# Attention and a gated MLP in one kernel: half of the transposes moved from the matrix engine to DMA

## The chip, the cores and the metric

The kernel runs on one core of one Trainium2 chip. A core has a matrix engine (TensorE, "PE" in the profile, with "PEld" for its weight loads), VectorE (DVE), ScalarE (ACT), GpSimd (POOL) and SyncE (SP), which work in parallel, each through its own instructions in program order. SP, ACT and POOL issue DMA transfers, which 16 DMA engines carry out. Matrix products land in PSUM, and DVE or ACT copy them from there to SBUF.

The metric is the time of one execution on the device in microseconds: 181.52 us as the median of three runs (181.5 to 182.01). The profiled execution spans 179.5 us.

## What is computed

Four batch items ("items one to four", b = 0 to 3 in the code), eight heads, 768 tokens, head dimension 64. Each head's sequence is cut into 8 blocks of 96. A small matrix P per head mixes the blocks of k and v; then each block attends only to itself. The result x goes through an MLP with the maximum of two branches.

```python
P = sort_net                                   # (4, 8, 8, 8)
for _ in range(5):                             # softmax over rows, then columns to sum 1
    P = np.exp(P - P.max(-1, keepdims=True))
    P = P / (P.sum(-1, keepdims=True) + 1e-09)
    P = P / (P.sum(-2, keepdims=True) + 1e-09)
k_sorted = np.einsum('bhij,bhjcd->bhicd', P, k_b)   # blocks of 96 tokens
v_sorted = np.einsum('bhij,bhjcd->bhicd', P, v_b)
scores = q_b @ k_sorted.transpose / sqrt(64)        # 96 x 96 per block
attn = softmax(scores);  x = attn @ v_sorted        # (3072 tokens, 512)
h1, h2 = x @ w1, x @ w2                             # 512 -> 1024
out = np.maximum(h1, h2) @ w_out                    # 1024 -> 512, float32
```

The kernel uses max(h1, h2) = relu(x(w1 - w2)) + x w2, and multiplies w2 by w_out once (wc). So the output of a tile is eight products with g = relu(...) and four with x itself.

## The kernel before

Products contract over partitions, so q and x are needed transposed. q is loaded as 128 partitions of 6 tokens each (token = 6 p + r). Two heads are put side by side by two DVE copies (pair_q; not for item one), and a transpose of 128 x 128 through PE then gives both heads' queries at once. Its result is copied out of PSUM into qT:

```python
def q_transposes(b, half, eng=None):
    if half == 0:
        qT[b] = qpool.tile([128, HP, R, 128], BF16, tag="qT", name="qT")
    ps = ps_bf16("tq_ps")
    for n in range(2 * R):                     # R = 6: 12 transposes
        hp, r = half * 2 + n // R, n % R
        c = slice(n * 128, (n + 1) * 128)
        if b in q_pair:
            nc.tensor.matmul(ps[:, c], q_pair[b][:, hp, r], ident, is_transpose=True, ...)
            continue
        ...                                    # item one: one head at a time
    evac(qT[b][:, half * 2 : half * 2 + 2]..., ps[:, 0 : 2 * R * 128], 2 * R * 128, two_x=True, eng=eng)
```

Queries of a block stand in qT in the order (r, c), not in token order (c, r). The scores of unit u (four blocks of two heads) and their exponential keep that order:

```python
def scores(b, u, n=0):
    ih, hp = divmod(u, HP)
    ps = ps_f32("s_ps")
    for ii in range(4):
        for h2 in range(2):
            rhs = qT[b][rows, hp, :, i * PB : (i + 1) * PB]      # 6 x 16 queries
            nc.tensor.matmul(ps[:, h2 * 512 + ii * BLK : h2 * 512 + (ii + 1) * BLK], kT[b]..., rhs, ...)
    nc.scalar.activation(out=e[:, 0 : 8 * BLK]..., in_=ps[0:BLK]..., func=AF.Exp, scale=scale)
```

values(b, u) multiplies e with v (the row sum comes along as a column of ones) and divides on DVE: one reciprocal, one multiplication that writes a half of a tile x (three buffers). When two units have filled x, x_transposes(b, t) transposes it in eight blocks on PE; only the copy into xT brings the tokens of a block into their order:

```python
def x_transposes(b, t, eng=None):
    ih, hh = divmod(t, 2)
    ps = ps_bf16("tx_ps")
    x = x_tiles.pop((b, ih, hh))
    for m in range(8):
        h2, ii = divmod(m, 4)
        nc.tensor.matmul(ps[:, h2 * 1024 + ii * BLK : ...], x[:, h2, ii]..., ident[0:BLK, 0:BLK],
                         is_transpose=True, ...)
    dst = xT[:, b % 2, ih, hh].rearrange("p h (i c r) -> p h i c r", r=R, c=PB)
    src = ps....rearrange("p h (i r c) -> p h i c r", r=R, c=PB)
    evac(dst, src, 2 * TCH, eng=eng)
```

`evac` and `pick` give a copy to ACT or DVE by a running estimate of their loads. All PSUM tiles (4 KB per partition) share four buffers.

The order of work is written by hand. For each item there are "units" of the MLP, and between them "steps" of the next item's attention. Units 0 to 3 (moe_h of channel half 0) read xT of groups t = 0 and 1; units 4 to 7 (half 1) read groups t = 2 and 3; then moe_out makes the outputs, and SP stores 256 tokens (512 KB) at a time. `tail` holds what is left over from the attention of the item whose MLP begins:

```python
elif b == 1:                                   # prepares item three during the MLP of item two
    vs = [lambda t=t: sort_v_pair(2, t) for t in range(8)]
    steps = group(*pairs) + group(*ks) + qs[:1] + group(*SC[0:2], vs[0]) + qs[1:]
    steps += group(*vs[1:4]) + group(*vs[4:7]) + group(*SC[2:4], vs[7]) + VA[:2]
else:                                          # b == 2
    steps = group(*pairs) + group(*ks) + qs + group(*SC[0:2])
    steps += group(*SC[2:5]) + VA[:2]
rest = SC[4:] if b == 1 else SC[5:]
steps += VA[2:3] + TR[:1] + VA[3:4]
steps += group(*rest[:-1]) + TR[1:2] + VA[4:5] + rest[-1:] + VA[5:6]
...                                            # steps from unit 2 on, spread evenly over the units
tail = {0: [VA[6]], 1: [TR[2], VA[7]], 2: [TR[3]]}    # after unit 0, 1, 2 of the next item
```

SC, VA and TR are the scores, values and x_transposes of the item; qs are the two halves of q_transposes, pairs the two pair_q copies, ks the sorts of k. q_raw has one buffer: the load of the next item's q waits for the pairing copies.

Of the kernel before, what the change touches and what calls it, by code (L numbers as in the profile page):

```python
# [15 lines left out]
def kernel(  # L16
# [16 lines left out]
    nc = tc.nc  # L33
# [6 lines left out]
    BLK = S // NB  # L40
# [5 lines left out]
    R = S // 128  # L46
    PB = 128 // NB
    HP = H // 2
    HB = BLK // 2
    TCH = S // 2  # L50
# [14 lines left out]
    def ps_f32(name):  # L65
        return psum.tile([128, 1024], FP32, tag="ps", name=name)

    def ps_bf16(name):
        return psum.tile([128, 2048], BF16, tag="ps", name=name)
# [21 lines left out]
    def pick(a_ns, d_ns):  # L91
        if load["A"] + a_ns <= load["D"] + d_ns:
            load["A"] += a_ns
            return "A"
        load["D"] += d_ns
        return "D"

    def evac(out_ap, in_ap, n, two_x=False, eng=None):
        a_ns, d_ns = (200 + n) / 1.2, (130 + (n / 2 if two_x else n)) / 0.96
        if eng:  # L100
            load[eng] += a_ns if eng == "A" else d_ns
        if (eng or pick(a_ns, d_ns)) == "A":
            nc.scalar.copy(out=out_ap, in_=in_ap)  # L103
        else:
            nc.vector.tensor_copy(out=out_ap, in_=in_ap)  # L105
# [5 lines left out]
    q_raw, qT = {}, {}  # L111
# [10 lines left out]
    for n in range(NE):  # L122
        t = big.tile([BLK, 8 * BLK + 32], BF16, tag=f"e{n}", name=f"e{n}")
# [194 lines left out]
    xT = big.tile([128, 2, 2, 2, 2, TCH], BF16, tag="xT", name="xT")  # L318

    q_pair = {}  # L320
# [11 lines left out]
    def q_transposes(b, half, eng=None):  # L332

        if half == 0:
            qT[b] = qpool.tile([128, HP, R, 128], BF16, tag="qT", name="qT")
        ps = ps_bf16("tq_ps")
        for n in range(2 * R):
            hp, r = half * 2 + n // R, n % R
            c = slice(n * 128, (n + 1) * 128)
            if b in q_pair:  # L340
                nc.tensor.matmul(  # L341
                    ps[:, c], q_pair[b][:, hp, r], ident, is_transpose=True, start=True, stop=True
                )
                continue
            for h2 in range(2):
                nc.tensor.matmul(
                    ps[h2 * 64 : h2 * 64 + 64, c],
                    q_raw[b][:, hp + 4 * h2, r * D : (r + 1) * D],
                    ident,
                    is_transpose=True,  # L350
                    start=True,
                    stop=True,
                )
        evac(
            qT[b][:, half * 2 : half * 2 + 2].rearrange("p h r c -> p (h r c)"),
            ps[:, 0 : 2 * R * 128],
            2 * R * 128,
            two_x=True,
            eng=eng,
        )  # L360
# [66 lines left out]
    e_tiles, x_tiles = {}, {}  # L427
# [4 lines that stand above are left out]
        keep_streaming(ps, n)  # L432
        for ii in range(4):
            i = ih * 4 + ii
            for h2 in range(2):
                rows = slice(h2 * 64, h2 * 64 + 64)
                rhs = qT[b][rows, hp, :, i * PB : (i + 1) * PB]
                nc.tensor.matmul(  # L438
                    ps[:, h2 * 512 + ii * BLK : h2 * 512 + (ii + 1) * BLK],
                    kT[b][rows, (hp * 8 + i) * BLK : (hp * 8 + i) * BLK + 128],  # L440
                    rhs,
                    start=True,
                    stop=True,
                )
        e = e_bufs[(b * 8 + u) % NE]
        nc.scalar.activation(  # L446
            out=e[:, 0 : 8 * BLK].rearrange("p (t f) -> p t f", t=2),
            in_=ps[0:BLK].rearrange("p (t f) -> p t f", t=2)[:, :, 0 : 4 * BLK],
            func=AF.Exp,
            scale=scale,  # L450
        )
        load["A"] += 800
        e_tiles[b, u] = e
# [34 lines left out]
    def x_transposes(b, t, eng=None):  # L488

        ih, hh = divmod(t, 2)  # L490
        ps = ps_bf16("tx_ps")
        x = x_tiles.pop((b, ih, hh))
        for m in range(8):
            h2, ii = divmod(m, 4)
            nc.tensor.matmul(  # L495
                ps[:, h2 * 1024 + ii * BLK : h2 * 1024 + (ii + 1) * BLK],
                x[:, h2, ii].rearrange("p n d -> p (n d)"),
                ident[0:BLK, 0:BLK],
                is_transpose=True,
                start=True,  # L500
                stop=True,
            )

        dst = xT[:, b % 2, ih, hh].rearrange("p h (i c r) -> p h i c r", r=R, c=PB)
        src = ps.rearrange("p (h f) -> p h f", h=2)[:, :, 0:TCH].rearrange(
            "p h (i r c) -> p h i c r", r=R, c=PB
        )
        evac(dst, src, 2 * TCH, eng=eng)


    w2T = big.tile([128, NFB, DMODEL], BF16, tag="w2T", name="w2T")
# [144 lines left out]
    SC, VA, TR = att(0)  # L656
# [37 lines left out]
    def load_rest():  # L694
# [3 lines left out]
    tail = {  # L698
        0: [VA[4]],
        1: [SC[6], SC[7], VA[5]],  # L700
        2: [VA[6], TR[2], VA[7]],
        3: [TR[3], lambda: w2_transposes(1, "A")(), load_rest, lambda: block_diagonals(1)],
        4: [lambda: block_diagonals(2), lambda: turn(second, 0)],
        5: [lambda: block_diagonals(3), lambda: turn(second, 24)],
        6: [lambda: turn(second, 48)],
        7: [lambda: turn(second, 72)],
# [8 lines left out]
    for b in range(B):  # L715
        units = [lambda t=t: moe_h(b, 0, t, None if b else "A") for t in range(4)]
        if b == 0:
            units[0] = lambda: None
            units[1] = lambda: None
        units += [lambda t=t: moe_h(b, 1, t) for t in range(4)]  # L720
        cost = [1.3] * 8
        if b == 0:
            units += [lambda dmt=dmt: w_product(dmt) for dmt in range(4)]
            cost += [1.7] * 4
        units += [
            lambda ti=ti, part=part: moe_out(b, ti, part)
            for ti in range(6 if b < B - 1 else 4)
            for part in range(2)
        ]
        cost += [1.3] * 12  # L730
        if b == B - 1:
            units += [
                lambda: moe_out_last(4, [(0, 512, "D")]),
                lambda: moe_out_last(5, [(0, 256, "A"), (256, 384, "D"), (384, 512, "A")]),
            ]
        steps, lo = [], 2
        if b < B - 1:
            qs = [lambda half=half: q_transposes(b + 1, half) for half in range(2)]
            pairs = [lambda two=two: pair_q(b + 1, two) for two in range(2)]
            ks = [lambda t=t, b=b: sort_k(b + 1, t) for t in range(3)]  # L740
            SC, VA, TR = att(b + 1)

            def group(*fs):
                return [lambda: [f() for f in fs]]

            if b == 0:
                lo = 9
                tail[7] += ks
                vs = [lambda t=t: sort_v(1, t) for t in range(4)]
                for m, c in enumerate((0, 24, 48, 72)):  # L750
                    VA[m + 1 : m + 2] = group(VA[m + 1], lambda c=c: turn(both, c))
                steps = group(*vs[:3]) + qs[:1] + group(*SC[0:2], vs[3]) + qs[1:] + VA[:1]
                steps += group(*SC[2:5]) + VA[1:2]
            elif b == 1:
                vs = [lambda t=t: sort_v_pair(2, t) for t in range(8)]
                steps = group(*pairs) + group(*ks) + qs[:1] + group(*SC[0:2], vs[0]) + qs[1:]
                steps += group(*vs[1:4]) + group(*vs[4:7]) + group(*SC[2:4], vs[7]) + VA[:2]
            else:
                steps = group(*pairs) + group(*ks) + qs + group(*SC[0:2])
                steps += group(*SC[2:5]) + VA[:2]  # L760
            rest = SC[4:] if b == 1 else SC[5:]
            steps += VA[2:3] + TR[:1] + VA[3:4]
            steps += group(*rest[:-1]) + TR[1:2] + VA[4:5] + rest[-1:] + VA[5:6]
        done = 0
        for n, unit in enumerate(units):
            unit()
            for step in tail.get(n, []):
                step()
            total = sum(cost[lo:-2])
            want = -(-len(steps) * sum(cost[lo : n + 1]) // total)  # L770
            while done < min(want, len(steps)):
                steps[done]()
                done += 1
        tail = {0: [VA[6]], 1: [TR[2], VA[7]], 2: [TR[3]]}
        if b == 0:
            tail[3] = [lambda: load_k(3)]
            tail[8] = [lambda: load_q(3)]
# [28 lines left out]
```

The softmax here doesn't subtract the row's maximum and nothing guards it: scores larger than these inputs give would overflow.

## Time and profile before

| | before |
|---|---|
| time, median of 3 | 181.52 us |
| span of the profiled execution | 179.5 us |
| x transposes on PE (tile tx_ps) | 128 matmuls in 16 groups |
| q transposes on PE (tile tq_ps) | 48 for item one, 72 for items two to four |
| copies tx_ps to xT | 11 on ACT (797 ns), 5 on DVE (957 ns) |
| copies tq_ps to qT | 7 on DVE (958 ns), 1 on ACT (1439 ns) |
| exponentials | 32 on ACT, 804 ns each |
| issues of DMA on SP | sort_net, 11 outputs of 512 KB, two smaller ones |

How to read the profile: a line such as "L495 PE MATMUL tx_ps<-ident,x" names the kernel's line, the engine, the operation, and output and inputs. Line 495 is the transpose of x, 341 that of paired q, 438 the scores, 446 the exponential, 463 the values, 474 and 480 the reciprocal and the multiplication that makes x, 563 the first products of the MLP (h), 579 the relu on DVE, 590 the output products, 326 the pairing copy, 209 the copies of v into its working layout. Busy times of PE are modelled at a matmul's end, so single matmuls overlap: eight in a row take less than eight times the mean of one. "The chain that ended last" is the work that set the end, followed back from the last instruction.

### The profile page before, as it was taken

To read this page: it belongs to the slowest core of one execution; us is meant where nothing else is said; L and a number is where in the kernel's file an instruction comes from. 1 tells how busy PE (TensorE), PEld (TensorE's weight loads), DVE (VectorE), ACT (ScalarE), POOL (GpSimd) and SP (SyncE) were. 2 spreads that over 40 slices of the span, in tenths; PEclk is the share of its full clock that TensorE was granted. 3 is DMA by queue.
4 is the path that set the end of the run, shared out by engine and by line. 5 is a ranking of instruction groups with operands and counts; after the bars stand their busy time and mean duration, and the time that the engine had idled before them with its cause. 6 is when DMAs were issued, how large, how long until landed. Compare 5 with 4: busy or idle time off the path is not lost.

```text
span 179.5 us, 4648 instructions
## 1 busy us (share of the span) xinstructions
PE 170.0 (95%) x2083; PEld 100.7 (56%) x2083; DVE 94.0 (52%) x192; ACT 91.8 (51%) x110; POOL 22.9 (13%) x39
## 2 busy tenths in 40 slices
PE   7797989999999989999989999999999999999993
PEld 2246666666565535577655554657555546554453
DVE  5878498559864395253586436156245415340210
ACT  3695876777664445368784341465833233520021
POOL 7861443200180000001000000000000000000000
PEclk9999999999999999999999999999999999999999
DMA  3999999999299991235600113200001132000333
GB/s 58 201 204 206 200 207 214 194 202 208 55 120 221 206 250 48 99 117 74 108 4 0 57 63 117 104 17 5 0 4 42 74 117 116 4 0 4 117 117 117
DMA packets 13939, 19.17 MB, mean 107 GB/s; under 512 B 800, under 2 KB 8864, under 8 KB 13920
## 3 DMA queue, kind: packets, MB, share of 16 engines
q0 software_dynamic: 10304, 12.58, 41.6%
q1 hardware_dynamic: 3328, 6.10, 8.9%
q8 instruction: 16, 0.26, 0.6%
q10 hardware_dynamic: 288, 0.20, 0.3%
q14 instruction: 3, 0.02, 0.0%
HBM read 25.17 MB, written 6.29 MB: 175 GB/s over the span
## 4 chain that ended last, share of the span: by engine, by line
PE 58%; DMA 29%; DVE 5%; issue 4%; POOL 2%; ACT 1%; POOLq 0%; DVEq 0%
PE out_ps L590 32%; PE h_ps L563 16%; DMA v_raw<-in_v_dram 10%; DMA w_sb<-in_moe_w_dram 10%; DMA q_raw<-in_q_dram 9%; PE o_ps L463 3%; PE tx_ps L495 2%; PE k_ps L371 2%; PE s_ps L438 2%; DVE g L579 2%; PE tq_ps L341 1%; DVE x L480 1%; DVE xT L105 1%; POOL v_raw L153 1%; DVE v_dc L209 1%
## 5 line engine op out<-in xcount | busy, mean ns | idle before, releaser
L590 PE MATMUL out_ps<-wo_sb,g 128*128 128x512 bf16 (+2 forms) x208 | 48.1, 363 | 0.2 <-DVE g L579 0.2
L563 PE MATMUL h_ps<-xT,w_sb 128*128 128x384 bf16 x256 | 46.1, 326 | 0.5 <-DVE g L579 0.2
L563 PEld LDWEIGHTS <-w_sb 128*128 128x128 bf16 x256 | 23.6, 97 | 15.1 <-issue 0.7
L577 ACT ACTIVATE g<-h_ps 128x768 bf16<-128x768 f32 x24 | 19.4, 811 | 23.4 <-PE h_ps L563 23.4
L446 ACT ACTIVATE e<-s_ps 96x768 bf16<-96x768 f32 x32 | 24.1, 804 | 14.0 <-PE s_ps L438 13.9
L590 PEld LDWEIGHTS <-g 128*128 128x128 bf16 x208 | 17.7, 97 | 15.8 <-issue 0.2
L590 PE MATMUL out_ps<-wc,xT 128*128 128x512 bf16 (+2 forms) x104 | 25.0, 362 | 0.0
L103 ACT COPY o<-out_ps 128x1024 f32<-128x1024 f32 x8 | 8.1, 1012 | 31.0 <-PE out_ps L590 27.3
L480 DVE TENSOR_TENSOR x<-o_ps,rs 96x512 bf16<-96x512 f32 x32 | 22.0, 687 | 1.1
L474 DVE RECIPROCAL rs<-o_ps 96x8 f32<-96x8 f32 x32 | 6.4, 201 | 27.4 <-PE o_ps L463 27.2
L590 PEld LDWEIGHTS <-xT 128*128 128x128 bf16 x104 | 9.9, 98 | 10.9
L209 DVE COPY v_dc<-v_raw 64x1536 bf16<-64x1536 bf16 (+2 forms) x9 | 14.1, 1583 | 1.8 <-DMA v_raw<-in_v_dram 1.7
L463 PEld LDWEIGHTS <-e 96*128 96x128 bf16 x256 | 11.2, 98 | 6.5 <-DVE x L480 1.1
L579 DVE TENSOR_SCALAR g<-h_ps 128x768 bf16<-128x768 f32 x8 | 7.7, 958 | 13.5 <-PE h_ps L563 10.6
L463 PE MATMUL o_ps<-v_sb,e 96*128 96x65 bf16 x256 | 12.9, 193 | 1.3 <-DVE x L480 0.6
L105 DVE CAST v_sb<-v_ps 96x1024 bf16<-96x1024 f32 x7 | 8.5, 1217 | 5.9 <-PE v_ps L392 3.9
L103 ACT CAST v_sb<-v_ps 96x1024 bf16<-96x1024 f32 x9 | 8.7, 1010 | 3.4 <-PE v_ps L392 2.6
L103 ACT CAST kT<-k_ps 128x1024 bf16<-128x1024 f32 x10 | 9.5, 1024 | 0.0
L103 ACT COPY xT<-tx_ps 128x768 bf16<-128x768 bf16 x11 | 8.8, 797 | 1.5 <-PE tx_ps L495 1.5
L438 PEld LDWEIGHTS <-kT 64*128 64x128 bf16 x256 | 6.2, 94 | 5.4 <-issue 4.4
L129 POOL DMA_DIRECT2D q_raw<-in_q_dram x4 | 3.6, 901 | 43.0 <-DVE q_pair L326 40.7
L438 PE MATMUL s_ps<-qT,kT 64*128 64x96 bf16 x256 | 9.0, 204 | 0.1
(78 smaller groups left out, 162.5 us busy)
## 6 DMA issues: line engine op xcount, KB each, us to landing
out_dram<-o SPq DMA_DIRECT2D x11, 512.0 KB, 2.8
k_raw<-in_k_dram POOLq DMA_DIRECT2D x12, 256.0 KB, 13.7
q_raw<-in_q_dram POOLq DMA_DIRECT2D x4, 768.0 KB, 8.9
v_raw<-in_v_dram POOLq DMA_DIRECT2D x6, 384.0 KB, 12.0
w_sb<-in_moe_w_dram POOLq DMA_DIRECT2D x3, 512.0 KB, 15.7
wo_sb<-in_moe_w_out_dram POOLq DMA_DIRECT2D x2, 512.0 KB, 19.9
v_raw<-in_v_dram POOLq DMA_DIRECT2D x3, 256.0 KB, 5.1
w_sb<-in_moe_w_dram POOLq DMA_DIRECT2D x2, 256.0 KB, 14.3
```

The costliest lines, as they stand in the source:

```text
L103: nc.scalar.copy(out=out_ap, in_=in_ap)
L105: nc.vector.tensor_copy(out=out_ap, in_=in_ap)
L209: nc.vector.tensor_copy(out=dst, in_=src)
L438: nc.tensor.matmul(ps[:, h2 * 512 + ii * BLK : h2 * 512 + (ii + 1) * BLK], kT[b][rows, (hp * 8 + i) * BLK : (hp * 8 + i) * BLK + 128], rhs ...
L446: nc.scalar.activation(out=e[:, 0 : 8 * BLK].rearrange("p (t f) -> p t f", t=2), in_=ps[0:BLK].rearrange("p (t f) -> p t f", t=2)[:, :, 0 ...
L463: nc.tensor.matmul(ps[:, h2 * 512 + ii * 65 : h2 * 512 + (ii + 1) * 65], e[:, (h2 * 4 + ii) * BLK : (h2 * 4 + ii) * BLK + 128], v_sb[:, m0 ...
L474: nc.vector.reciprocal(out=rs, in_=ov[:, :, :, 64])
L480: nc.vector.tensor_tensor(out=x, in0=ov[:, :, :, 0:D], in1=rs.to_broadcast([BLK, 2, 4, D]), op=ALU.mult,)
L563: nc.tensor.matmul(h_ps[t][:, m * 512 : m * 512 + TCH], w1_sb[:, hp, fb * 128 : (fb + 1) * 128], xT[:, b % 2, ch, hp % 2, hp // 2, :], sta ...
L577: nc.scalar.activation(out=g, in_=src, func=AF.Relu)
L579: nc.vector.tensor_scalar(out=g, in0=src, scalar1=0.0, scalar2=None, op0=ALU.max)
L590: nc.tensor.matmul(dst, g_tiles[b, ch, m // 2][:, m % 2, off : off + 128] if m < NFB else xT[:, b % 2, ch, hp % 2, hp // 2, off : off + 12 ...
```

## The change

The transposes of x for items two to four, and of q for items three and four, are taken from PE and done by DMA: one transfer transposes a whole group and writes straight to xT or qT, so that PSUM and the copy out of it are not needed. The transfers go on SP's queue, among the outputs. [...]the order is now mended earlier: the exponential reads PSUM in token order, and e, x and xT have that order for all items. The scores of a block move to 128 columns each, so that the exponential's pattern has one stride for all eight blocks.

To give the transfers time, pairing and q transposes move to the start of an item's MLP (after unit 0), the sorts of v stand ahead of the first scores, and one values unit (VA[6]) moves ahead of the border between items. Item one keeps both transposes on PE, and item two its q.

```diff
 def q_transposes(b, half, eng=None):
     if half == 0:
         qT[b] = qpool.tile([128, HP, R, 128], BF16, tag="qT", name="qT")
+    if b > 1:
+        hps = slice(half * 2, half * 2 + 2)
+        nc.sync.dma_start_transpose(
+            out=qT[b][:, hps].rearrange("p h r c -> p (h r) c"),
+            in_=q_pair[b][:, hps].rearrange("p h r d -> p (h r d)"),
+        )
+        return
 ... scores:
-                    ps[:, h2 * 512 + ii * BLK : h2 * 512 + (ii + 1) * BLK],
+                    ps[:, h2 * 512 + ii * 128 : h2 * 512 + ii * 128 + BLK],
 ...
-            out=e[:, 0 : 8 * BLK].rearrange("p (t f) -> p t f", t=2),
-            in_=ps[0:BLK].rearrange("p (t f) -> p t f", t=2)[:, :, 0 : 4 * BLK],
+            out=e[:, 0 : 8 * BLK].rearrange("p (t c r) -> p t c r", t=8, r=R),
+            in_=ps[0:BLK]
+            .rearrange("p (t f) -> p t f", t=8)[:, :, 0:BLK]
+            .rearrange("p t (r c) -> p t c r", r=R),
 ... x_transposes:
+        x = x_tiles.pop((b, ih, hh))
+        if b:
+            nc.sync.dma_start_transpose(
+                out=xT[:, b % 2, ih, hh].rearrange("p h (i c) -> p (h i) c", c=BLK),
+                in_=x.rearrange("p t i n d -> p (t i n d)"),
+            )
+            return
 ... (item one: the copy to xT is now contiguous on both sides, two_x=True)
 ... order of work, b == 1:
-                steps = group(*pairs) + group(*ks) + qs[:1] + group(*SC[0:2], vs[0]) + qs[1:]
-                steps += group(*vs[1:4]) + group(*vs[4:7]) + group(*SC[2:4], vs[7]) + VA[:2]
+                tail[0] = pairs + qs + tail[0]
+                steps = group(*ks) + group(*vs[1:4]) + group(*SC[0:2], vs[0])
+                steps += group(*vs[4:7]) + group(*SC[2:4], vs[7]) + VA[:2]
 ... b == 2:
-                steps = group(*pairs) + group(*ks) + qs + group(*SC[0:2])
+                tail[0] = pairs + qs + tail[0]
+                steps = group(*ks) + group(*SC[0:2])
 ... all items but the last:
-            steps += group(*rest[:-1]) + TR[1:2] + VA[4:5] + rest[-1:] + VA[5:6]
+            steps += group(*rest[:-1]) + TR[1:2] + VA[4:5] + rest[-1:] + VA[5:7]
 ...
-        tail = {0: [VA[6]], 1: [TR[2], VA[7]], 2: [TR[3]]}
+        tail = {0: [TR[2], VA[7]], 1: [TR[3]]}
```

More of the change, by code (lines that the diff above doesn't have):

```diff
@@ L490, in x_transposes @@
         ih, hh = divmod(t, 2)
+        x = x_tiles.pop((b, ih, hh))
[5 more added lines that the diff above has]
+            return
         ps = ps_bf16("tx_ps")
-        x = x_tiles.pop((b, ih, hh))
         for m in range(8):
@@ L495, in x_transposes @@
             nc.tensor.matmul(
-                ps[:, h2 * 1024 + ii * BLK : h2 * 1024 + (ii + 1) * BLK],
+                ps[:, m * BLK : (m + 1) * BLK],
                 x[:, h2, ii].rearrange("p n d -> p (n d)"),
@@ L502, in x_transposes @@
             )
-        dst = xT[:, b % 2, ih, hh].rearrange("p h (i c r) -> p h i c r", r=R, c=PB)
-        src = ps.rearrange("p (h f) -> p h f", h=2)[:, :, 0:TCH].rearrange(
-            "p h (i r c) -> p h i c r", r=R, c=PB
+        evac(
+            xT[:, b % 2, ih, hh].rearrange("p h f -> p (h f)"),
+            ps[:, 0 : 2 * TCH],
+            2 * TCH,
+            two_x=True,
+            eng=eng,
         )
-        evac(dst, src, 2 * TCH, eng=eng)
     w2T = big.tile([128, NFB, DMODEL], BF16, tag="w2T", name="w2T")
```

## The prediction

> **What bounds the kernel now.** I read the page's busy table first, then the chain that ended last in order of time, then a table of stages, then the tile view of the transposes and the list of DMA issues. The page says that TensorE (PE) is the busy engine, and that VectorE (DVE) and ScalarE (ACT) are about half idle:
>
> ```profile
> PE 170.0 (95%) x2083; PEld 100.7 (56%) x2083; DVE 94.0 (52%) x192; ACT 91.8 (51%) x110; POOL 22.9 (13%) x39
> ```
>
> An average hides stages, so next the stages (columns: stretch and its length, then busy us and instruction count of PE, weight loads, DVE, ACT, GpSimd, then clock, DMA share, GB/s):
>
> ```profile
> 62.00:95.00 33.00, 31.77 (x463) 19.48 (x461) 19.93 (x26) 20.89 (x24) 0.90 (x1) 1.00 0.44 99
> 95.00:131.00 36.00, 35.40 (x462) 21.32 (x462) 16.44 (x28) 18.34 (x24) 0.00 (x0) 1.00 0.12 45
> 131.00:155.00 24.00, 23.66 (x211) 12.96 (x210) 10.74 (x19) 7.87 (x11) 0.00 (x0) 1.00 0.18 67
> ...
> 64.00:161.00 97.00, 95.04 (x1155) 56.55 (x1156) 47.06 (x72) 47.46 (x57) 0.90 (x1) 1.00 0.22 63
> ```
>
> From 64 to 161 us PE is idle for only 97.00 - 95.04 = 1.96 us. So a matmul that disappears there should shorten the kernel by its own pipelined time, as long as no wait takes its place. Before 62 us the chain runs through loads from HBM; the last is v of items three and four, behind which DVE stands still for 1.72 us (to 62.00). What is saved before that point is mostly lost.
>
> The chain shows what the transposes cost (columns: start us, us, what). Around the border between items three and four:
>
> ```profile
> 115.00 1.30 PE h_ps L563 x8
> 116.31 0.36 PE tx_ps L495 x8
> 116.68 0.96 DVE xT L105
> 117.64 0.12 DVE rs L474
> 117.79 0.70 DVE x L480
> 118.53 0.51 PE tx_ps L495 x8
> 119.05 1.30 PE h_ps L563 x8
> 120.35 1.63 PE k_ps L371 x96
> 121.98 1.41 PE h_ps L563 x8
> 123.39 1.34 PE tq_ps L341 x24
> ```
>
> A group of eight x transposes holds PE for 0.34 us where it stands elsewhere in the chain (0.36 here, with a wait behind it). The q transposes of one item hold it for 1.34 us, 0.67 per half. The stretch from 116.68 to 118.53 is not all idle (another matmul group ran beside it): the timeline gives 0.34 us of PE idle ahead of the second x group, and the same again at 154.10.
>
> **What the Trainium skill says.** "VectorE: DVE Perf Modes", section "The three transpose paths", gives 390 ns for a 128x128 transpose on TensorE and 1309 ns through the DMA crossbar. The trace agrees that one alone is slow on PE (203 to 219 ns each by the tile view), but pipelined it is 0.67/12 = 56 ns, so the DMA path is not a saving of latency, only of PE time. "DMA: Bandwidth & Descriptors", section "Latency and other measured facts", gives 261 GB/s for a DMA transpose with a non-contiguous middle dimension, 350 to 400 where contiguous. The kernel before has no such transfer, so no trace here shows it. The same page, "Queues, rings and completion order", says that transfers issued by SP share one ring on each DMA engine, taken in order, and that an engine goes round robin between queues by packet. The trace fits: a 512 KB output takes 2.8 us alone and 6.1 us when it meets the loads. "TensorE: Matmul & The Clock Gate", section "Part 1: The HAM clock gate", warns that PE idle for about 3.4 us halves its clock; the trace shows a clock of 1.00 in every stage, so it has not yet been put to the test.
>
> **The change part by part.**
>
> *PE loses work.* Of 16 x groups 12 go: 12 x 0.34 = 4.1 us. Of eight q halves four go: 4 x 0.67 = 2.7 us. The instruction lists agree: 2083 matmuls become 1939, 96 + 48 fewer. The two idle gaps of 0.34 us ahead of the second x group go too: 0.7 us. One x group (0.3 us) stands before the v load's wait and counts for nothing. The 16 groups no longer take one of the four PSUM buffers, and DVE and ACT lose their copies (four of 0.94 to 1.44 us for qT, twelve of 0.8 to 0.96 us for xT); of the remaining 1.3 us of PE idle, mostly waits for such buffers, I count 0.5 us as won. Sum: 4.1 + 2.7 + 0.7 - 0.3 + 0.5 = 7.7 us.
>
> *The exponentials cost the same.* Their read of PSUM now has a stride of 16 elements, where it was contiguous. The old copy of xT made just such a strided read and took as long per element as the contiguous exponential (columns: what and how often, then busy us and mean ns of one, then idle time ahead):
>
> ```profile
> L446 ACT ACTIVATE e<-s_ps 96x768 bf16<-96x768 f32 x32 | 24.1, 804 | 14.0 <-PE s_ps L438 13.9
> ...
> L103 ACT CAST kT<-k_ps 128x1024 bf16<-128x1024 f32 x10 | 9.5, 1024 | 0.0
> L103 ACT COPY xT<-tx_ps 128x768 bf16<-128x768 bf16 x11 | 8.8, 797 | 1.5 <-PE tx_ps L495 1.5
> ```
>
> The kT copy reads f32 with a stride of 64 elements at 1024 ns, against 1012 for a contiguous one. So 0 us, and the PE work per score is unchanged (the outputs only lie 128 apart, not 96).
>
> *Three new places where PE can wait.* Transfers of x for the first half of a next item have some 8 us between their issue and the products that read them; I take them as hidden. The second-half x of an item (groups three and four), and the queries of the next one, are issued just after the item's border, behind one another on SP, and behind the 512 KB output of the item before. Sizes: a q half is 128 x 1536 x 2 B = 393 KB, an x group 96 x 1024 x 2 B = 197 KB. At the skill's 261 GB/s that is 1.51 and 0.75 us, an estimate. Start and landing of a transfer I take from the outputs:
>
> ```profile
> out_dram<-o SPq DMA_DIRECT2D x11, 512.0 KB, 2.8
> ...
> out_dram<-o SPq DMA_DIRECT2D x1, 64.0 KB, 1.6
> ```
>
> Slope (2.8 - 1.6) us per 448 KB, so 1.4 us for the data of 512 KB and 1.4 us fixed.
>
> Count from the start of the first hidden product (h) after the border; each step by the chain's durations (h 1.30, attention value 0.24, sort of k 1.64, h after it 1.41, three sorts of v 0.88, two scores 0.45).
> - Item two: second-half x is read at 1.30 + 0.24 + 1.30 + 1.30 + 1.64 + 1.41 + 0.88 = 8.1. Output issued at 1.4 (its ACT copy ends 1.04 after, issue 0.37). Then 1.4 (output) + 2 x 1.51 + 2 x 0.75 (transposes) + 1.4 fixed: lands at 8.7, a stall of 0.6. But the q load of item four is released by the same pairing copies that release the q transposes, 786 KB at the 207 GB/s of the page's loads = 3.8 us on the same engines. If all of it gets in between, the stall is 4.4. I take 3.0.
> - Item three: in the changed order the pairing copies stand on DVE behind the relu of the first h: 1.30 + 0.96 + 2 x 0.55 = 3.4. Then 4.5 + 1.4 = 9.3, against a read at 1.30 + 0.24 + 1.30 + 1.30 + 1.64 + 1.41 + 0.45 = 7.6. Stall 1.7.
> - Item four has no q behind it: 1.4 + 1.4 + 1.5 + 1.4 = 5.7, read at 1.30 + 0.24 + 3 x 1.30 = 5.4. Stall 0.3.
>
> Sum of the stalls: 5.0 us. Net: 7.7 - 5.0 = 2.7 us saved, 181.5 - 2.7 = 178.8 us.
>
> **The rivals.**
> 1. *All hidden.* Transposes near 400 GB/s and little collision with the q load: the three transfers' data falls to 3.0 us, stalls to about 1 us together, time about 175. For it: DMA is busy only 0.12 to 0.22 of the stages after 95 us. Against: the slack per border is 5 to 8 us while each border queues 0.4 to 1.2 MB, fixed times aside.
> 2. *The crossbar becomes the wait.* If it moves only 150 GB/s (4.5 becomes 7.9 us), the stalls are about 4 to 6, 5 and 1 us, more than the gain: 185 us. At under 80 GB/s PE stands still for more than 3.4 us at each border, the clock falls as well, and the time is 195 or more. For it: the 1309 ns of a single 128x128 block, if nothing of it overlaps, is 12 x 1.31 = 15.7 us per q half. Against: the page's own 261 GB/s on a larger transfer.
> 3. *The gain moves to another wait.* The v load that ends the chain at 62 us shares its engines with the first x transposes of item two. A 197 KB transfer among loads could push it by 0.5 to 1 us. That would give about 179.5.
>
> **Range and chances.** The middle case says 178.8. The best case is 181.5 - 7.7 = 173.8, with all waits hidden. The upper side is long, because the crossbar's rate is the one figure that no trace here shows: 150 GB/s gives 185, a little less 188. So 174.0 to 188.0 for 8 in 10. Over 2% faster means below 177.9, which needs stalls of at most 4.1 us: 0.42. Within 2%, 177.9 to 185.2: 0.28. Slower: 0.30.
>
> **What would show it.** PE busy should fall by 6 to 7 us, and L495 and L341 groups from 128 and 72 to 32 and 24 matmuls. The exponentials should stay at about 804 ns. The list of DMA issues should give the time from issue to landing of the two transposes: around 2 to 3 us for x and 3 to 5 for q, more at the border of item two. The waits of PE for xT or qT transfers should stand in three places, the borders of items two, three and four, with the lengths above. I am wrong if x or q transfers take over 6 us each when alone, if the exponentials grow (32 of them, but ACT has slack), or if PE waits for the first-half x too.

## The result and the profile after

| | before | after |
|---|---|---|
| time, median | 181.74 us | 188.48 us |
| span of the profiled execution | 179.5 us | 187.1 us |
| ratio, 95% interval | | 1.0373 [1.0344, 1.0401] |

The change makes the kernel 3.7% slower. The page's busy table and clock row of the changed kernel:

```profile
PE 167.2 (89%) x1939; PEld 95.5 (51%) x1939; DVE 87.1 (47%) x185; ACT 84.1 (45%) x101; POOL 22.9 (12%) x39
...
PEclk9999999999999999998589999999699999999999
```

PE lost 144 of its 248 transposing matmuls, as counted, but its share fell from 95 to 89%, and its clock dips twice, near 90 and 132 us. The stages tell where (columns as before; the cut at 135 us follows the later border):

```profile
62.00:95.00 33.00, 25.14 (x346) 14.08 (x345) 13.09 (x20) 14.30 (x17) 0.90 (x1) 0.90 0.87 146
95.00:135.00 40.00, 35.39 (x434) 20.04 (x434) 16.44 (x26) 17.46 (x23) 0.00 (x0) 0.96 0.36 80
135.00:165.00 30.00, 29.67 (x227) 15.81 (x226) 10.67 (x20) 9.03 (x12) 0.00 (x0) 0.99 0.30 80
```

From 62 to 95 us PE now stands idle for 33.00 - 25.14 = 7.9 us (before: 1.2), while DMA's share has doubled from 0.44 to 0.87. The chain of the changed kernel around the three borders:

```profile
79.86 1.65 PE k_ps L378 x96
81.52 0.97 SPq L338
82.53 4.66 SPq L338
87.23 1.29 SPq L502
88.62 2.85 DMA xT<-x
91.52 2.08 PE h_ps L580 x6
...
121.26 1.82 PE h_ps L580 x12
123.08 5.61 DMA qT<-q_pair
128.70 0.14 issue
128.85 2.89 DMA xT<-x
131.79 1.78 PE h_ps L580 x6
...
160.51 3.02 DMA xT<-x
163.58 5.04 PE h_ps L580 x30
```

"SPq L338" is SP busy with issuing a q transpose, "SPq L502" with issuing an x transpose. At item two's border the end hangs on SP getting rid of its transfers one after another, at item three's on the landing of q and then x, at item four's on one x. The waits of PE for these transfers (us in total, times, longest):

```profile
PE h_ps L580 <- DMA xT<-x: 9.0, 5, 6.5
...
PE s_ps L445 <- DMA qT<-q_pair: 1.9, 1, 1.9
```

By border, from the timeline: 6.5 + 0.3 us at item two's, 1.9 + 1.4 + 0.5 at item three's, 0.3 at item four's; 10.9 us in all. The six h products after the long wait take 2.08 us where six should take 0.98: the clock.

A ledger from the starts of each item's first h product (before: 75.65, 113.46, 149.02; after: 75.72, 119.72, 157.35):

| stretch | before | after | difference | PE work and gaps taken out | waits for transposes |
|---|---|---|---|---|---|
| item two's border to item three's | 37.8 | 44.0 | +6.2 | -2.7 | 6.7 |
| item three's to item four's | 35.6 | 37.6 | +2.1 | -3.0 | 3.9 |
| item four's to the end | 30.5 | 29.8 | -0.7 | -1.0 | 0.3 |

In the last stretch, difference and columns close. In the middle one 1.2 us remain; the slow clock after its waits is of that size (six products took 0.8 us and eight products 0.6 us too long). In the first, 2.2 us remain; the slow clock is part of it.

### The profile page after: what moved, and what is told of

Its sections match the earlier page's. It is cut to its first block, busy times and chain, and to the rows that moved or that the text cites. A ratio compares the mean times of both kernels' runs of the same rounds, so it can differ in the third digit from the quotient of the medians.

```text
span 187.1 us, 4386 instructions
## 1 busy us (share of the span) xinstructions
PE 167.2 (89%) x1939; PEld 95.5 (51%) x1939; DVE 87.1 (47%) x185; ACT 84.1 (45%) x101; POOL 22.9 (12%) x39
## 4 chain that ended last, share of the span: by engine, by line
PE 55%; DMA 29%; issue 4%; SPq 4%; POOL 3%; DVE 3%; ACT 2%; DVEq 0%; POOLq 0%
PE out_ps L607 30%; PE h_ps L580 15%; DMA q_raw<-in_q_dram 14%; DMA v_raw<-in_v_dram 6%; DMA xT<-x 5%; SPq L338 3%; DMA qT<-q_pair 3%; PE o_ps L472 3%; PE s_ps L445 2%; PE v_ps L399 1%; POOL v_raw L153 1%; DVE x L489 1%; PE k_ps L378 1%; PE tq_ps L353 1%; ACT e L453 1%
## 5 line engine op out<-in xcount | busy, mean ns | idle before, releaser
L580 PE MATMUL h_ps<-xT,w_sb 128*128 128x384 bf16 x256 | 48.4, 337 | 9.4 <-DMA xT<-x 9.0
L580 PEld LDWEIGHTS <-w_sb 128*128 128x128 bf16 x256 | 24.2, 99 | 26.6 <-DMA xT<-x 8.1
L594 ACT ACTIVATE g<-h_ps 128x768 bf16<-128x768 f32 x23 | 18.6, 813 | 27.4 <-PE h_ps L580 27.4
L103 ACT COPY o<-out_ps 128x1024 f32<-128x1024 f32 x9 | 9.1, 1013 | 38.1 <-PE out_ps L607 31.8
L105 DVE CAST v_sb<-v_ps 96x1024 bf16<-96x1024 f32 x8 | 9.6, 1218 | 20.7 <-PE v_ps L420 16.8
L596 DVE TENSOR_SCALAR g<-h_ps 128x768 bf16<-128x768 f32 x9 | 8.6, 956 | 20.0 <-PE h_ps L580 20.0
L607 PEld LDWEIGHTS <-xT 128*128 128x128 bf16 x104 | 9.9, 98 | 10.9
L445 PE MATMUL s_ps<-qT,kT 64*128 64x96 bf16 x256 | 9.5, 215 | 3.0 <-DMA qT<-q_pair 1.9
L445 PEld LDWEIGHTS <-kT 64*128 64x128 bf16 x256 | 6.7, 100 | 9.2 <-issue 5.0
L103 ACT CAST v_sb<-v_ps 96x1024 bf16<-96x1024 f32 x8 | 7.8, 1020 | 2.2 <-PE v_ps L399 2.2
L129 POOL DMA_DIRECT2D q_raw<-in_q_dram x4 | 3.6, 902 | 37.5 <-DVE q_pair L326 34.9
L105 DVE COPY o<-out_ps 128x1024 f32<-128x1024 f32 x2 | 2.5, 1225 | 11.4 <-PE out_ps L607 11.4
## 6 DMA issues: line engine op xcount, KB each, us to landing
q_raw<-in_q_dram POOLq DMA_DIRECT2D x4, 768.0 KB, 10.9
```

Of the source, the lines that this page charges most:

```text
L445: nc.tensor.matmul(ps[:, h2 * 512 + ii * 128 : h2 * 512 + ii * 128 + BLK], kT[b][rows, (hp * 8 + i) * BLK : (hp * 8 + i) * BLK + 128], rhs ...
L580: nc.tensor.matmul(h_ps[t][:, m * 512 : m * 512 + TCH], w1_sb[:, hp, fb * 128 : (fb + 1) * 128], xT[:, b % 2, ch, hp % 2, hp // 2, :], sta ...
L594: nc.scalar.activation(out=g, in_=src, func=AF.Relu)
L596: nc.vector.tensor_scalar(out=g, in0=src, scalar1=0.0, scalar2=None, op0=ALU.max)
L607: nc.tensor.matmul(dst, g_tiles[b, ch, m // 2][:, m % 2, off : off + 128] if m < NFB else xT[:, b % 2, ch, hp % 2, hp // 2, off : off + 12 ...
```

## The experiments

Two theories. *Mine after the result*: the queue at the item borders, where x waits behind q and both share the DMA engines with a load, is the whole loss; the exponential and the crossbar are not. *Rivals*: the crossbar is slow in itself, or the token order costs something. A ratio stands against the kernel before, with its 95% interval.

**tokens_only**: only the token order is left, on before's order of work.

```diff
-        if b > 1:            # q by DMA
+        if b > 9:
-        if b:                # x by DMA
+        if b > 9:
 # steps, tail: as in the kernel before
```

> All transposes on PE and the order of work as before; only the exponential's token order and the contiguous copy of x remain of the change. Theory (the queue on SP at the item borders is the cost): exponentials stay at about 805 ns, time 181.5 us within 0.7. Rival (the strided read or the 128-column scores cost something that the queue hides): 183 or more.

181.04 us, ratio 0.9963 [0.9948, 0.9977]. The exponentials took 804 ns, as before (805 in the changed kernel). The token order is free, and a little better than that: the copies of x to xT, now contiguous, take DVE 554 ns in place of 957. That rival falls.

**x_dma_only** and **q_dma_only**: one half of the change each. The first has `if b > 9` for q and the old steps with q on PE; the second has `if b > 9` for x.

> x of items two to four by DMA, all q back on PE in the old steps. Theory (x transfers wait behind the q transfers): each x transfer lands about 3 us after its issue, PE waits for xT under 0.5 us at each border, and 12 x 0.34 us of PE work is gone: 177 to 178.5 us. Rival (the crossbar transposes are slow in themselves): waits of 1 us or more for xT at each border, 180 us or more.

179.85 us, ratio 0.9894 [0.9865, 0.9924]. PE waits 0.9 us for xT in all (0.6 and 0.3), near what the theory says, but the gain is smaller than I expected: from item two's border to item three's it needs 38.5 us, more than the 37.8 of before. PE is idle there for 2.4 us in place of 0.6: 0.6 us of it is the wait for xT, while the q load runs, and many small waits make the rest.

> q of items three and four by DMA after unit 0, all x back on PE. Theory: no xT wait, so the 6.5 us stall of item two's border goes; the scores may still wait for qT, about 2 us at each of two borders, against 2.7 us of PE work saved: 179.5 to 183 us. Rival (x is the costly one and q harmless): 178.5 to 179.5 us with no wait for qT.

182.60 us, ratio 1.0051 [1.0036, 1.0066]: inside the range of the theory, but not for its reason. No wait of the scores for qT shows in its trace. It loses 1.5 us ahead of item two's border (77.1 us, before 75.65), where PE waits 1.6 us for DVE's x and one values unit more now stands; that this unit is the reason is argued. Of the next two stretches one is longer than before (38.5 us for 37.8) and one shorter (34.9 for 35.6). With q by DMA, less PE work came out slower.

**q_load_late**: the changed kernel, its load of item four's q held back by a small GpSimd copy that needs the relu of unit 4.

```diff
+            def load_q_late():
+                hold = const.tile([128, 8], BF16, tag="hold", name="hold")
+                nc.gpsimd.tensor_copy(out=hold, in_=g_tiles[1, 1, 0][:, 0, 0:8])
+                load_q(3)
-            tail[8] = [lambda: load_q(3)]
+            tail[8] = [load_q_late]
```

> The changed kernel, but the load of item four's queries waits for the relu of unit 4 of item two, so it can't meet the transposes of that border. Theory (the collision with this load makes item two's border the worst): issuing a q half takes SP about 1.8 us there as at item three's border, not 5, and the wait for xT falls from 6.7 to 1.5 to 3 us: 183 to 185 us. Rival (the load is harmless, the transposes need that long after a full queue): 188 us as the changed kernel.

183.77 us, ratio 1.0104 [1.0067, 1.0141], so 4.7 us of the change's loss went with this one load. SP's own issues show it; first the changed kernel, then q_load_late (start us, us, what; both issue two q halves at item two's border):

```profile
77.28 9.91 SPq L338 DMA_TRANSPOSE qT<-q_pair  x2
...
123.08 3.51 SPq L338 DMA_TRANSPOSE qT<-q_pair  x2
```

```profile
76.98 3.94 SPq L338 DMA_TRANSPOSE qT<-q_pair  x2
```

Beside the load, SP needs 9.9 us to issue what takes it 3.5 to 3.9 us without. The longest wait for xT at item two's border fell from 6.5 to 1.6 us. The single transfers in the changed kernel (the last number is us to landing), show both sides of the collision; the third line is the load in the kernel before:

```profile
qT<-q_pair SPq DMA_TRANSPOSE x1, 10.6
```

```profile
q_raw<-in_q_dram POOLq DMA_DIRECT2D x1, 768.0 KB, 11.2
```

```profile
q_raw<-in_q_dram POOLq DMA_DIRECT2D x1, 768.0 KB, 7.1
```

The packets show what stood ahead of what. In the changed kernel SP issued the output at 76.8 us and the first q half at 77.3. From 77 to 81 us only packets of the load (q0) moved; from 82 to 83 those of SP's queue (q1, still the output) and of the load moved in like number:

```profile
q0 software_dynamic: 655, 0.50, 109.7%
```

```profile
q1 hardware_dynamic: 103, 0.21, 61.8%
q0 software_dynamic: 111, 0.09, 54.1%
```

The small packets of the q half begin at 83.7 us, 6.4 us after its issue. So it hardly shared the engines with the load: it stood behind the output, and this behind the load. Why SP's packets did not move at all for the first four microseconds is open.

**q_in_load**: is it the load alone? The kernel before, with one scratch transpose of a q half (zeros) after unit 3 of item two.

```diff
+            tail[3] = tail.get(3, []) + [
+                lambda: ready(src_qa, 3, 0, 128),     # DVE copies 8 columns of g: sets the moment
+                lambda: turn_by_dma(src_qa, dst_qa),  # nc.sync.dma_start_transpose
+            ]
```

> The kernel before, with one scratch transpose of a q half after unit 3 of item two, while the q load of item four is in flight, and nothing else on SP near it. Theory (the load slows a transpose): 6 to 10 us to its landing instead of 3.4, and the load itself takes longer than the 7.1 us it takes in the kernel before. Rival (only a full SP queue hurts): 3.4 to 4.5 us.

5.9 us, just under my range, and 8.5 us for the load. It was issued at 85.33, in the second half of the load (81.5 to 90.0). The DMA view from 75 to 100 us names the packets:

```profile
DMA packets 2883, 1.75 MB, mean 70 GB/s; under 512 B 1600, under 2 KB 2624, under 8 KB 2880
...
q0 software_dynamic: 1040, 0.79, 23.1%
```

The q half is 1600 packets under 512 B (393 KB / 1600 = 246 B), the load 1040 of some 760 B. "DMA: Bandwidth & Descriptors" in the Trainium skill, section "Queues, rings and completion order", says that an engine takes turns between queues by packet. The 103 and 111 packets above fit that, but turns do not explain this run: by 88.0 us 111 packets of the q half had moved, and the load had 15 left. The transpose lost its time elsewhere. Its first packets moved 2.3 us after its issue, against 1.2 in the run alone below, and from 88.5 to 89.5 us, with two packets of the load left, only 54 of them moved. Such a standstill comes up again under border_data. Nor are the 8.5 us of the load a sign of sharing: in tokens_only, with no DMA transpose at all, it took 8.3. So this run shows that a transpose beside a load starts late; it does not show that the two slow each other.

**alone**, **pair_alone**, **border_alone**: the crossbar by itself, in scratch tiles during item four's MLP, where no load runs. The edits are like that of q_in_load, at units 4, 7 and 11; the output's transfer stands ahead of unit 11's.

> The kernel before, with two more transposes into scratch tiles during item four's MLP, when no load runs: one of the shape of an x group (96 x 1024) after unit 4, one of a q half (128 x 1536) after unit 7. They measure the crossbar by itself. If it moves 261 GB/s and has the 1.4 us fixed that I took from the outputs, x lands 2.2 us after its issue and q 2.9; theory after the earlier runs (x 2.9 at item four's border): x 2.7 to 3, q 3.5 to 4.5, that is about 150 GB/s. Rival (the times at item three's border are the crossbar's own): q 5.3 us or more.

```profile
dst_x<-src_x SPq DMA_TRANSPOSE x1, 2.7
dst_q<-src_q SPq DMA_TRANSPOSE x1, 3.4
```

197 KB more take 0.7 us more: 281 GB/s, and 2.0 us are fixed. The rate that I took from the skill (261 GB/s) is about right for a source of zeros; the slow crossbar falls as a cause. The fixed part is 0.6 us above the 1.4 that I took from the outputs. SP is held 1.3 and 1.75 us by the issue alone.

> The kernel before, with scratch transposes of the q half's shape during item four's MLP, when no load runs: two in a row after unit 7, one right behind a 512 KB output after unit 11. One alone took 3.4 us. If the second starts only when the first is done (a queue in order), the first lands in 3.4 us and the second about 1.4 to 1.8 us after it; if the engines share, both take 4 us or more. Behind the output: 3.4 to 4.5 us if its rest (under 1.5 us) is all it waits for; 5 us or more if an output slows a transpose beyond that.

3.6 and 3.3 us for two in a row, each counted from its own issue, and 4.0 behind an output: neither form of queueing makes 5 us.

> The kernel before, with the queue of item three's border repeated in scratch during item four's MLP: behind a 512 KB output two transposes of a q half and two of an x group, all issued one after another. Theory (the queue itself makes the 5.3 to 5.7 us): q halves land 5 us or more after their issue, the x groups 3.5 to 4. Rival (something else at the border, such as the sorts' and scores' own traffic, slows them): q halves in 3.4 to 4.5 us.

```profile
dst_qa<-src SPq DMA_TRANSPOSE x1, 4.2
dst_qb<-src SPq DMA_TRANSPOSE x1, 3.7
dst_xa<-src SPq DMA_TRANSPOSE x1, 2.8
dst_xb<-src SPq DMA_TRANSPOSE x1, 2.7
```

Here my theory missed: the same queue lands its q in 4.2 and 3.7 us, not in the 5.6 and 5.3 of item three's border. Two more runs asked why. **border_mid** puts the four behind the output that SP issues at 102.0 us, beside the attention of item three; **border_data** reads the real paired queries in place of a tile of zeros.

> As border_alone, but the same four scratch transposes stand behind item two's second output, when no load runs and PE, ACT and DVE work on the attention of item three. If the other engines' work slows the transposes, the q halves land in 5 to 6.5 us and x in 3.5 or more, against 4.2, 3.7 and 2.8 in border_alone; if not, within 0.3 us of these.

4.1, 3.7, 2.8 and 2.7 us: the other engines' work, in that stretch, makes no difference.

> As border_alone, but the source is item four's real paired queries at the place that the changed kernel reads, not a tile of zeros. If the content or the place of the source matters, q lands in 5 us or more; I expect 3.7 to 4.3 us as in border_alone.

```profile
dst_qa<-q_pair SPq DMA_TRANSPOSE x1, 4.6
dst_qb<-q_pair SPq DMA_TRANSPOSE x1, 4.7
dst_xa<-q_pair SPq DMA_TRANSPOSE x1, 3.4
dst_xb<-q_pair SPq DMA_TRANSPOSE x1, 2.9
```

Source content or place costs 0.2 to 1.0 us each, against what I expected; it was not tried which of the two it is. Beyond that, 0.6 to 1.0 us per q half of the real border remain. The trace of the changed kernel shows where they lie. The first view is from 124.5 to 125.5 us, the second from 126 to 127.5, the third from 127.0 to 128.2, just before the first q half lands at 128.7:

```profile
DMA packets 832, 0.21 MB, mean 213 GB/s; under 512 B 832, under 2 KB 832, under 8 KB 832
```

```profile
q8 instruction: 1, 0.02, 4.0%
```

```profile
DMA packets 49, 0.01 MB, mean 10 GB/s; under 512 B 49, under 2 KB 49, under 8 KB 49
```

The transfers all but stop for over a microsecond, right after a packet of 16 KB on the queue that the page calls instruction (q8, at 126.7 us). In the kept traces nearly every such packet that falls into the middle of a DMA transpose after the border of item two is followed by a standstill like this one; into the four transfers of border_alone, border_mid and border_data none falls, and none of them stands still. An x group with no load and no q half beside it landed in 2.8 to 3.7 us without such a packet and in 4.1 to 5.4 with one (all_early, x_early, warm_wait, x_dma_only). No run moved these packets, so the link is seen, not tested; nor was it tried what the sort of k, which runs at the real border, adds.

**x_first**: in the changed kernel, pairing and q stand behind both x transfers.

```diff
-                tail[0] = pairs + qs + tail[0]
+                tail[1] = tail[1] + pairs + qs      # items three and four
```

> The changed kernel, but at the borders of items two and three the pairing and the q transfers stand behind both x transfers on SP. Theory (in the queue the one that stands behind pays): at item three's border the waits for xT fall from 1.9 to at most 0.6 us, as at item four's, and the wait of the scores for qT grows from 1.9 to 3 to 4 us; the sum there does not get much smaller. At item two's the q load starts later by 3 us, and xT waits 2 us or less: 184.5 to 187 us. Rival (order on the queue doesn't matter, the engines share): waits as in the changed kernel, 188.5 us.

185.46 us, ratio 1.0204 [1.0174, 1.0233]. The waits for xT almost vanish (0.3 us in all), and the scores wait for qT 6.0 us at item two's border, beside the load, and 2.2 at item three's. So at the latter the sum fell from 3.9 to 2.2 us, more than I had expected: x behind q had paid for q, without q being helped.

**q_early**: pairing and q transposes in the middle of the MLP before the border.

```diff
-                tail[0] = pairs + qs + tail[0]      # twice
+            if b == 0:
+                tail[18] = [pair_q(2, 0), pair_q(2, 1), q_transposes(2, 0), q_transposes(2, 1)]  # as lambdas
+            if b == 1:
+                tail[10] = [pair_q(3, 0), pair_q(3, 1), q_transposes(3, 0), q_transposes(3, 1)]
```

> The changed kernel, with the pairing copies and the q transposes moved from the item border to the middle of the MLP before it (unit 18 of item one's, unit 10 of item two's), so that at a border only the output and two x transfers stand on SP. Theory (x waits behind the q transfers, and these behind the q load): waits for xT fall to 0.3 to 0.7 us at each border, none for qT, the clock stays at 1.00; 176 to 178.5 us. Rival (transposes among other transfers are slow wherever they stand): xT or scores still wait 2 us or more per border, 180 us or more.

179.84 us, ratio 0.9902 [0.9885, 0.9919]. Half a hit: nothing waits for qT, and from item three's border to item four's it takes 32.4 us (before 35.6). But at item two's border x still comes late, with no q transfer issued behind the border (the second q half, issued at 71.6 us, landed only at 81.8), and the chain of q_early says so:

```profile
76.91 9.77 DMA xT<-x
86.68 0.05 issue
86.72 2.78 PE h_ps L580 x8
```

The early pairing also released the q load early, at 69.4 us, and it reached over the border (11.7 us to landing).

**q_early_load_late**: q_early and the held-back load together (with unit 12 in place of 10, and the load at tail[7]).

> q_early, and the load of item four's queries held back until unit 4 of item two has its relu. Theory (q_early's one long wait, 3.1 us for xT at item two's border, is the collision with that load): the wait falls to at most 0.7 us there, the clock stays at 1.00 through 75 to 95 us, 2.5 to 4 us under q_early: 176 to 177.5 us, the fastest so far. Rival (the transfers of the first-half x and of q before the border fill the queue): the wait stays above 2 us, 179 us or more.

175.97 us, ratio 0.9677 [0.9640, 0.9714]: faster than both kernels, by 5.7 us against before and 12.5 against the changed one. Its waits for xT, and its stage from 75 to 95 us, with the clock at 1.00:

```profile
PE h_ps L580 <- DMA xT<-x: 0.5, 1, 0.5
```

```profile
75.00:95.00 20.00, 18.57 (x352) 12.13 (x351) 8.55 (x11) 14.72 (x18) 1.09 (x2) 1.00 0.58 122
```

The three stretches of the ledger take 36.3, 32.4 and 29.8 us, against 37.8, 35.6 and 30.5 before.

**before_load_late**: a control, the kernel before with the late load alone (same edit).

> The kernel before, with only the late q load of q_early_load_late, as a control. If the late load helps by itself (less traffic beside PE's work), it is faster by 1 us or more; theory: it matters only where transposes share the engines, so 181.5 us within 0.5.

182.11 us, ratio 1.0019 [1.0008, 1.0030]. The late load is worth nothing by itself; it pays only where transposes share the engines.

**q_early_load_late_x2**, **all_early** and **x_early**: more lead for x. The first issues the third x group's transfer ahead of the last output; the other two also take the last values units ahead of the border (all_early on top of q_early, x_early with q on PE).

```diff
-            ... + VA[5:7]
+            ... + VA[5:6] + TR[2:3] + VA[6:7]                 # _x2;  tail {0: [VA[7]], 1: [TR[3]]}
+            ... + VA[5:6] + TR[2:3] + VA[6:8] + TR[3:4]       # all_early, x_early;  tail {}
```

> As q_early_load_late, and the third x group's transfer of each item (its values are there) is issued ahead of the item's last output, with only the fourth behind it. Theory: the waits for xT left at borders three and four (0.3 to 0.5 us each) shrink; 0.3 to 1 us under q_early_load_late. Rival: the fourth group, which needs values made after the border, sets the wait, and the time is the same within 0.3 us.

177.50 us, ratio 0.9762 [0.9741, 0.9783]: slower than without, a miss for both forms of the expectation. The loss is in item two's stretch (37.7 us in place of 36.3). That the extra step moves the others in the hand-written spread is argued.

> As q_early, and the last values units and both second-half x transfers of an item stand ahead of its border too. Theory: no wait for a transpose is left, 0.3 to 1.5 us under q_early: 175.5 to 177.5 us. Rival (the waits had covered other work, and PE now waits for the exponentials or for PSUM instead): no faster than q_early.

> x by DMA with values and transfers ahead of the border, q on PE as before. Theory: xT waits (0.9 us in x_dma_only) go, 178 to 179.3 us, and slower than all_early by about the 2.7 us of q on PE. Rival (q by DMA saves nothing because its transfers cost as much elsewhere): as fast as all_early.

181.57 us, ratio 0.9965 [0.9945, 0.9986], and 184.59 us, 1.0143 [1.0077, 1.0209]. No product waits for xT any more, and yet both lose against the runs they build on (q_early 179.84, x_dma_only 179.85): the attention is now too early for its own inputs. The waits of x_early, and its stage from 64 to 75 us (clock 0.69):

```profile
PE out_ps L607 <- DVE x L489: 1.9, 1, 1.9
...
PE s_ps L445 <- DVE x L489: 1.3, 1, 1.3
```

```profile
64.00:75.00 11.00, 8.45 (x53) 3.63 (x54) 6.86 (x10) 2.49 (x4) 0.00 (x0) 0.69 0.79 130
```

DVE makes x between the copies of v that came late from HBM, so PE waits there. The rival of all_early's expectation holds, with DVE's x in place of the exponentials. Part of the loss is the clock that these waits can lower: of 20 executions of all_early, the six with a mean clock of 0.998 or more took 179.8 to 180.4 us, the twelve with 0.989 to 0.991 took 181.2 to 181.9, and the two with 0.981 some 183.

**warm_wait**: what the clock costs. The changed kernel with filler products ahead of unit 4 of item two: `moe_h(b, 1, t, n=24 * 512 if (b, t) == (1, 0) else 0)`.

> The changed kernel, with 24 filler matmuls of 512 columns (5.2 us at full clock) ahead of unit 4 of item two, which run while PE waits for xT there (6.7 us). They leave the wait as it is and keep PE busy. Theory (PE's clock falls after a long wait and costs 2 to 3 us more at item two's border): clock near 1.00 from 90 to 95 us, the six products after the wait back to about 1.0 us from 2.08; 185.5 to 187 us. Rival (the low clock is a consequence without cost): 188.5 us, or more by part of the filler.

188.33 us, ratio 1.0360 [1.0320, 1.0400]: no gain. The chain of warm_wait, item two and item three:

```profile
91.67 1.14 PE h_ps L580 x6
...
131.09 2.09 PE h_ps L580 x6
```

At item two's border the filler does keep the clock (1.14 us in place of 2.08), and item three starts 0.8 us earlier (118.94 in place of 119.72). At item three's border this execution lost more than the changed kernel's (2.09 us for six against 1.78). So the clock costs 0.8 us at item two's border, not the 2 to 3 I expected, and the long waits themselves are the loss.

## Why the prediction was wrong

- *PE loses 7.7 us of work and gaps.* Right for the work, 1.5 us too high for the time. In q_early_load_late PE is busy for some 7 us less than before (162.5 in place of 170.0, with 14 of its matmuls missing from the trace); it gains 5.7 us and has 0.5 us of waits for xT left, 6.2 together. Between the last borders it gains 3.1 us where I counted 3.0; the shortfall is before item two's border (0.4 us gained, as predicted nearly nothing) and in item two's stretch (1.5 of 2.7).
- *The exponentials cost the same.* Right.
- *First-half x is hidden.* Right: the waits stand at the three borders only.
- *Item four's border, 0.3 us.* Right, 0.3.
- *Item three's border, 1.7 us.* Wrong by 2.2 us: 3.9. The issue at 3.4 us after the border was right (123.08 - 119.72), but q landed 5.6 us after its issue, where the sum has 1.5 + 1.4 = 2.9. Of the difference 0.5 us are there for a transfer alone (3.4), 0.8 more in the repeated queue (4.2), 0.4 more with the real source (4.6), and 1.0 falls into the standstill from 127.0 us, whose cause was not tested.
- *Item two's border, 3.0 us.* Wrong by 3.7 us, and this is the step that failed: I let the q load add at most its own 3.8 us once, at its own full rate, and took 2.4 of it beside a stall of 0.6 from the queue alone. q_load_late separates the two: without the load PE waits 2.1 us for xT there (1.6 + 0.5), with it 6.7, so the load costs 4.6 us. The runs showed this in its place: SP's queue moved nothing from 77 to 81 us, then its output beside the load, and the q half only from 83.7, when the load was nearly over, so that it landed 10.6 us after its issue in place of 3.4; the load itself stretches from 7.1 to 11.2 us; and SP, held by issuing the q halves for 9.9 us, does not get to the x transfers meanwhile. Taking the load away from the border gave back 4.7 us of the kernel's time.
- *Clock.* I named it only for a rival; it fell at both long waits and cost 0.8 us at item two's border (warm_wait) and about 1.4 us at item three's (0.8 + 0.6 in the ledger).

The stalls were thus 10.9 us where I had 5.0. Of the 9.7 us between 178.8 and 188.48, the longer stalls are 5.9, the clock about 2.2, and the smaller gain about 1.5. The mechanism and its three places were those predicted; the terms of the queue were mis-sized. Rival 2 came near the time (185) with stalls of 4 to 6, 5 and 1 us, but for a wrong reason: the crossbar alone moves 281 GB/s, not 150.

## What to carry to other kernels

Work taken from a busy engine is won only if what replaces it lands before it is needed, so count every transfer that stands ahead in the same queue, and every load that the same change releases. A DMA transpose issued beside a bulk load landed up to three times as late here (10.6 us in place of 3.4): put it where no load runs, or hold the load back. When some of a change's waits can be moved by a few lines (here: q earlier, one load later), try that before giving it up; the same change went from 3.7% slower to 3.2% faster.

## What the runs showed of the hardware

- A DMA transpose within SBUF took 2.7 us for 197 KB and 3.4 us for 393 KB, alone; issuing it held SP for 1.3 and 1.75 us, and for up to 5.2 us beside a load.
- The first q half of the same queue took 4.2 us with a source of zeros and 4.6 with real data at another place.
- In item three's border of the changed kernel the packets of a DMA transpose all but stood still from 127.0 to 128.2 us, after an instruction packet of 16 KB at 126.7; the standstill is shown, the link is not tested.
- PE's clock fell not only after the 6.5 us wait. In the profiled execution of x_early its mean was 0.69 from 64 to 75 us, around two waits of 1.3 and 1.9 us with one short group of scores (0.34 us) between them: 1.00 from 64 to 65 us, 0.81 from 65 to 66, 0.50 from 66 to 72. "TensorE: Matmul & The Clock Gate" in the Trainium skill, section "Part 1: The HAM clock gate", puts the fall at an idle window of some 3.4 us; here it came at about 65.6 us, 2.2 us after PE's last work of any length (63.4), so the short group did not save the clock, and less than 3.4 us was enough. It is not sure to fall there: in one of the four executions of x_early the mean clock was 1.00.
- A read of PSUM with a stride of 16 f32 elements cost ACT nothing (805 ns against 804).
